# Postmix products with 112 weight columns, and the first loads of stage 1 moved into the last slots of attention

## The chip, the cores and the metric

The kernel runs on one core of one Trainium2 chip. The metric is the device time of one execution in microseconds (us); lower is better. A core has TensorE (PE for its products, PEld for its weight loads), VectorE (DVE), ScalarE (ACT), GpSimd (POOL) and SyncE (SP), each with an instruction queue that is worked off in order, and 16 DMA engines that all queues share.

## What is computed

Three layers, one after the other, on fp32 data (`w_in` and `w_out` of the second arrive as 64-bit floats):

```
scores = q @ k.T / 8                      # 4 batches, 12 heads, 448 x 448, head size 64
scores = einsum('bhij,hg->bgij', scores, w_pre)
attn   = softmax(scores, axis=-1)
attn   = einsum('bhij,hg->bgij', attn, w_post)
x      = (attn @ v) -> 1792 x 768
h = x @ w_in; g = h - tanh(h)             # 768 -> 2048
x = g @ w_out                             # 2048 -> 768
logits = x @ phi                          # 32 slots
d = softmax over tokens; slot_in = d.T @ x
slot_out[e] = relu(slot_in[e] @ w1[e]) @ w2[e]   # 8 experts, 4 slots each
out = softmax over slots(logits) @ slot_out
```

## The kernel before, in words

**Attention** (`talking_heads`) works on 16 chunks of 120 or 88 queries of one batch. A chunk's scores are computed per pair of heads (`scores`, L279) and copied to SBUF by ACT (`keep`, L287). A chunk is then cut into slots of 10 queries x 12 heads = 120 rows; there are 184 slots, and the loop at L579 takes one per turn of `s`. Two slots make a pair, and the work of a pair is:

- `regroup(s + 4)` (L304, on SP): a DMA that brings the score rows of one slot to the tile `D`, head by head. It is issued four slots, two pairs, ahead of its use, into one of six `D` buffers.
- `premix(s)` on even slots: products of `D` with `w_pre` (tile `pm`, L313), then the negated row maximum on DVE (`mx`, L317).
- `expo(s)`: exp on ACT with the row sums (`e`, L325); `guard`, `recip`, `norm`: POOL and DVE turn the sums into post-mixing weights `wk`, 60 columns for 12 heads x 5 queries (L331, L335, L342).
- `postmix(s - 4)`: products of `e` as weights with `wk` as moving operand (tile `tm`, L356). The result has keys on partitions. The 448 keys are 4 groups `c` of 112 (`JP`), and each group is cut in two halves `z` of 56 (`JH`), one at partition 0 and one at partition 64. So one product has 64 rows and 56 weight columns, and there are 2 x 4 x 2 x 2 = 32 per pair. An fp32 product is two instructions of TensorE, so that is 64 matmuls and 64 weight loads per pair. TensorE runs the four quarters of its array side by side.
- `gather(s - 1 - 4)` on odd slots: ACT copies `tm` to the tile `aT` (L370 to L374).
- `values` (tile `vx`, L395): products of `v` with `aT`; DVE copies `vx` to `xs` in `rest` (L405), which the loop puts behind the next `premix` (list `late`); a DMA takes `xs` to `xd` in HBM, input of stage 1.

Which slot gets the scores of a later chunk (`head`), the transposes of keys (`k_pair`, tile `kx`) and queries (`q_half`, tile `qx`), `values`, and loads is planned ahead of the loop from estimated loads per slot. Because `z` leaves gaps at partitions 56 to 63 and 120 to 127, the tiles for `v` (`vns`) and `tms` are set to zero there ahead of the loop (L536, L538 on DVE, L546 on POOL), and `load_v` needs two DMAs per half batch. Beside attention, `Conversion` turns `w_in` and most of `w_out` from 64-bit to 32-bit floats: a DMA into one of five `f64` buffers, steps on ACT, DVE and POOL (last a sum on POOL, L71), a store to HBM.

**Stage 1** (`moe_and_slots`) is a generator that attention starts as `follow()` at slot 180, after the pool of attention's early tiles is closed. It runs up to its next `yield` at each `next(more)`. The first run (end of slot 180) issues loads of four units of `w_in` (`load_w`, L776, 384 KB each) and of `x` (`load_x`, L819, three parts). The next runs come between the last postmixes and gathers: `split_w(0)` and `split_x` cut fp32 into two parts (ACT copy and DVE subtraction, L787, L788, L823, L824), five products that only keep TensorE busy (`warm`, L1197), then the products of step 0 (`product`, tile `hp`, L840) two column groups at a time, and the gate (`gate_act`, `gate_first`, `gate_last`). `save_w` stores split weights through ACT's queue (L801). From step 2 on each of 64 steps has 18 products, and weights of the experts are loaded as buffers come free; the last 80 us run the experts and the output.

Of the kernel before, what the change touches and what calls it, by code (L numbers as in the profile page):

```python
# [17 lines left out]
NP = NH // 2  # L18
NR = 4
JP = SEQ // NR  # L20
JH = JP // 2
IH = 5
# [51 lines left out]
class Conversion:  # L74
    def __init__(self, nc, w_in, w_out, wi, wo):
        self.nc, self.w_in, self.w_out, self.wi, self.wo = nc, w_in, w_out, wi, wo
        self.KD = w_in.shape[0] // 128
        self.CV = w_out.shape[1] // 2
        self.pool = None
        self.bufs = 5  # L80
        self.adder = nc.gpsimd
        self.t = {}

    def load(self, j):
        f, hf, o = j
        r = self.pool.tile([128, self.CV, 2], I32, tag="f64", name="f64", bufs=self.bufs)
# [46 lines left out]
def talking_heads(tc, ident, q, k, v, w_pre, w_post, xd, box, follow):  # L133
# [17 lines left out]
    er = early_stack.enter_context(tc.tile_pool(name="at_early", bufs=2))  # L151
    cv.pool = er
    psq = early_stack.enter_context(tc.tile_pool(name="at_psq", bufs=2, space=PSUM))

# [6 lines left out]
    def load_k(b, p):  # L161
        t = er.tile([JP, 2, NR, HD], FP32, tag="kn", name="kn", bufs=NP)
        nc.sync.dma_start(out=t, in_=k[b, 2 * p:2 * p + 2].rearrange("e (p r) d -> p e r d", r=NR))
        nat_k[b, p] = t

    def load_v(b, hf):
        t = vns[(2 * b + hf) % 3]
        src = v[b, hf * NP:(hf + 1) * NP].rearrange("h (p r) d -> p h r d", r=NR)
        for z in range(2):
            nc.sync.dma_start(out=t[64 * z:64 * z + JH], in_=src[JH * z:JH * z + JH])  # L170
        nat_v[b, hf] = t
# [175 lines left out]
    def postmix(s):  # L347
        es, wks = e_t.pop(s), wk_t.pop(s)
        xs = tms
        for x in range(2):  # L350
            for c in range(NR):
                for i in range(2):
                    for z in range(2):
                        h = slice(64 * i, 64 * i + 64)
                        j = JP * c + JH * z
                        nc.tensor.matmul(  # L356
                            xs[i][64 * z:64 * z + JH, x, c], lhsT=es[x][h, j:j + JH], rhs=wks[x][h],
                            start=True, stop=True)
        tm_t[s] = xs

    def gather(s):
        for i, x in enumerate(tm_t.pop(s)):
# [3 lines left out]
            c0 = sum(z for q, z in chunks[n][3] if q < o)  # L366
            out = attn_t[n].rearrange("p r h i -> p (r h) i")
            x = x.rearrange("p x r h i -> p (r h) x i")
            if m == 2 * IH:
# [14 lines left out]
    def values(n, g):  # L384
# [6 lines left out]
        for i in range(2):  # L391
            for c in range(NR):
                for e in range(2):
                    h = 4 * g + 2 * i + e
                    nc.tensor.matmul(  # L395
                        x[64 * e:64 * e + 64, i, :ni], lhsT=nat_v[b, h // NP][:, h % NP, c, :], rhs=a[:, c, h, :ni],
                        start=(c == 0), stop=(c == NR - 1))
# [136 lines left out]
    tms = [ps.tile([128, 2, NR, NH, IH], FP32, tag=f"t{i}", name="tm", bufs=1) for i in range(2)]  # L534
    for z in range(2):
        nc.vector.memset(vns[0][64 * z + 32:64 * z + 64], 0.0)  # L536
    for t in tms:
        nc.vector.memset(t, 0.0)  # L538

    for p in range(3, NP):  # L540
        load_k(0, p)
    for t in ds:
        nc.gpsimd.memset(t[:4], 0.0)
    for t in vns[1:]:
        for z in range(2):
            nc.gpsimd.memset(t[64 * z + 32:64 * z + 64], 0.0)  # L546
    for _ in range(WARM):
# [23 lines left out]
    for a in at.get(("head", -1), []):  # L571
        for f in scores4(*a):
            f()
    halves = []
    late = []
# [3 lines left out]
    while s < NS:  # L579
# [38 lines left out]
        for f in box["setup"][s - 6:s - 5] if s >= 6 else []:  # L618
            f()
        if s == NS - D_AHEAD:  # L620
            early_stack.close()
            more = follow()
            next(more)
# [19 lines left out]
def moe_and_slots(tc, ident, xd, wi, wo, wo4, wis, consts, w1, w2, out, box):  # L643
# [33 lines left out]
    psums = ExitStack()  # L677
    keep = whole.enter_context(tc.tile_pool(name="m_keep", bufs=1, reuse_waits="tile"))
    rgp = whole.enter_context(tc.tile_pool(name="m_ring", bufs=1, reuse_waits="tile"))
    xap = whole.enter_context(tc.tile_pool(name="m_xa", bufs=1, reuse_waits="tile"))  # L680
    xep = firsts.enter_context(tc.tile_pool(name="m_xe", bufs=1, reuse_waits="tile"))
    ph = psums.enter_context(tc.tile_pool(name="m_h", bufs=1, space=PSUM))
    bank_pool = {"h0": ph, "h1": ph}

# [3 lines left out]
    def r32(ap):  # L688
        return ap.bitcast(F32R)

    ceK = keep.tile([128, NBL, NSL], FP32, tag="ceK", name="ceK")
# [4 lines left out]
    rg = rgp.tile([128, 2 * RU], FP32, tag="rg", name="rg")  # L696
    rgs = rgp.tile([128, 2 * RU], FP32, tag="rgs", name="rg")
    xbuf = {0: [xap.tile([128, XW], FP32, tag=f"x{l}", name="xa") for l in range(2)]}
    quad, quad_a, quad_b = [xep.tile([128, FB * NRM], FP32, tag=f"quad{i}", name="quad") for i in range(3)]
    ring = [w.rearrange("p (m h i) -> p m h i", m=2, h=2) for w in (rg[:, :RU], rg[:, RU:], rgs[:, :RU], rgs[:, RU:])]  # L700

    def unit(t):
        return ring[t % 4] if t < THREE else ring[(4, 0, 1)[(t - THREE) % 3]]

# [93 lines left out]

    def save_w(t):
        if t < NF:  # L800
            nc.scalar.dma_start(out=wis[t], in_=unit(t))  # L801

# [6 lines left out]
    def load_x(p):  # L809
# [6 lines left out]
        dst = dst.rearrange("p (a s) -> p a s", a=KD)  # L816
        step = KD if p else 2
        for a in range(0, KD, step):
            nc.sync.dma_start(out=dst[:, a:a + step], in_=xd[p][:, a:a + step])  # L819

# [274 lines left out]
    def step(t):  # L1095
# [75 lines left out]
        if b == NPASS - 2 and f == NF - 1:  # L1171
            mem["slow"] = True
            for l in range(2):
                give(xap.tile([128, EXB], FP32, tag=f"x{l}", name="ex"))
        if b == NPASS - 1:
# [300 lines left out]
def fused_kernel(  # L1476
# [40 lines left out]
    def side(hf):  # L1517
# [14 lines left out]
        "late": [j for j in order if j[2] and j[0] >= LATE],  # L1532
    }
    with tc.manual_schedule():
        talking_heads(
# [31 lines left out]
```

## Time and profile before

| what | us |
|---|---|
| median of 3 runs (lowest, highest) | 891.73 (885.24, 895.21) |
| the profiled execution | 886.23 |
| its span, first to last instruction | 884.5 |
| attention up to the last premix | 0 to 434 |
| last postmixes and values, begin of stage 1 | 434 to 458 |
| steps of stage 1 | 458 to 775 |
| slots and experts | 775 to 884 |

The profile is of one execution; all rows below are of that one. Busy times of TensorE contain the time in which a product passes through the array: a group of 64 short matmuls begins one every few ns, each takes some 0.2 us. In rows of products, 64*56 is rows x weight columns, and 64x60 the moving operand.

### The profile page before, as it was taken

To read this page: it belongs to the slowest core of one execution; us is meant where nothing else is said; L and a number is where in the kernel's file an instruction comes from. 1 tells how busy PE (TensorE), PEld (TensorE's weight loads), DVE (VectorE), ACT (ScalarE), POOL (GpSimd) and SP (SyncE) were. 2 spreads that over 40 slices of the span, in tenths; PEclk is the share of its full clock that TensorE was granted. 3 is DMA by queue.
4 is the path that set the end of the run, shared out by engine and by line. 5 is a ranking of instruction groups with operands and counts; after the bars stand their busy time and mean duration, and the time that the engine had idled before them with its cause. 6 is when DMAs were issued, how large, how long until landed. Compare 5 with 4: busy or idle time off the path is not lost.

```text
span 884.5 us, 28648 instructions
## 1 busy us (share of the span) xinstructions
PE 807.9 (91%) x11790; PEld 570.8 (65%) x11790; DVE 556.7 (63%) x1181; ACT 570.5 (64%) x1345; POOL 247.7 (28%) x428
## 2 busy tenths in 40 slices
PE   8889988799987999899899999999999999999965
PEld 6556665566665667566676667667776786964322
DVE  5357766577666777788456986566765777830104
ACT  4777887687776878798666776546664666821103
POOL 5234344334334444454303452000000003700000
PEclk9999999899999999999999999999999999999988
DMA  9787888768888788785759976678764457899998
GB/s 182 191 234 220 213 236 248 218 190 211 231 253 226 219 206 239 236 254 177 256 176 363 374 260 223 207 316 317 302 215 175 149 179 256 313 359 413 424 392 303
DMA packets 131766, 224.53 MB, mean 254 GB/s; under 512 B 44852, under 2 KB 112436, under 8 KB 128052
## 3 DMA queue, kind: packets, MB, share of 16 engines
q1 hardware_dynamic: 128288, 209.84, 74.8%
q10 hardware_dynamic: 3348, 12.87, 3.7%
q8 instruction: 93, 1.52, 0.7%
q14 instruction: 37, 0.30, 0.1%
HBM read 147.96 MB, written 36.18 MB: 208 GB/s over the span
## 4 chain that ended last, share of the span: by engine, by line
PE 50%; DMA 18%; ACT 13%; DVE 12%; issue 5%; SPq 1%; POOL 1%; ACTq 0%; POOLq 0%; DVEq 0%
PE hp L840 21%; DMA D<-S 7%; DMA ex<-in_moe_w_dram 7%; ACT e L325 6%; PE pm L313 5%; PE sc L279 5%; DVE mx L317 4%; PE vx L395 3%; PE tm L356 3%; PE gt L911 2%; ACT S L287 2%; PE kx L236 2%; PE lgp L995 2%; PE sp L1077 1%; ACT aT L370 1%
## 5 line engine op out<-in xcount | busy, mean ns | idle before, releaser
L325 ACT ACTIVATE e<-pm,mx 128x448 f32<-128x448 f32 x184 | 115.1, 631 | 86.3 <-DVE mx L317 84.9
L840 PE MATMUL hp<-xa,rg 128*128 128x512 f32 x576 | 152.7, 405 | 0.2 <-POOL rg L788 0.2
L317 DVE TENSOR_REDUCE mx<-pm 128x1 f32<-128x448 f32 x184 | 106.1, 618 | 73.5 <-PE pm L313 73.4
L356 PEld LDWEIGHTS tm<-wk,e 64*56 64x56 f32 x5888 | 104.7, 128 | 62.8 <-issue 32.4
L356 PE MATMUL tm<-wk,e 64*56 64x60 f32 x5888 | 113.5, 216 | 13.3 <-issue 7.9
L313 PE MATMUL pm<-D,wpre 64*64 64x448 f32 (+2 forms) x736 | 107.6, 565 | 18.4 <-DMA D<-S 15.2
L840 PEld LDWEIGHTS hp<-xa,rg 128*128 128x128 f32 x576 | 102.3, 188 | 28.9 <-issue 10.5
L287 ACT ACTIVATE S<-sc 120x448 f32<-120x448 f32 (+1 forms) x186 | 91.4, 553 | 4.6 <-PE sc L279 3.0
L279 PE MATMUL sc<-khi,qT 64*120 64x448 f32 (+1 forms) x384 | 83.6, 392 | 9.3 <-DVE xs L405 6.2
L342 POOL TENSOR_SCALAR wk<-wpost,rv 128x60 f32<-128x60 f32 x184 | 86.9, 503 | 16.5 <-DVE rv L335 13.8
L331 POOL TENSOR_SCALAR rv<-ss 128x2 f32<-128x2 f32 x92 | 24.5, 266 | 225.3 <-ACT e L325 194.6
L395 PE MATMUL vx<-aT,vn 128*64 128x120 f32 (+1 forms) x1536 | 83.9, 262 | 2.0 <-ACT S L287 1.3
L797 POOL TENSOR_TENSOR rg<-rg 128x384 fp32r<-128x384 f32 x24 | 23.9, 1012 | 208.8 <-DVE rg L794 205.0
L395 PEld LDWEIGHTS vx<-aT,vn 128*64 128x64 f32 x1536 | 74.7, 137 | 7.2 <-issue 3.0
L860 ACT ACTIVATE sq<-hp 128x512 f32<-128x512 f32 (+1 forms) x62 | 32.9, 530 | 68.0 <-PE hp L840 68.0
L370 ACT ACTIVATE aT<-tm 128x480 f32<-128x480 f32 x144 | 75.8, 593 | 0.1
L871 DVE SCALAR_TENSOR_TENSOR qd<-qd,sq 128x512 f32<-128x512 f32 (+1 forms) x61 | 37.6, 616 | 59.1 <-ACT mk L867 53.7
L840 PE MATMUL hp<-xb,rg 128*128 128x512 f32 x288 | 74.7, 404 | 0.0
L840 PEld LDWEIGHTS hp<-xb,rg 128*128 128x128 f32 x288 | 52.1, 188 | 16.6 <-issue 6.3
L279 PEld LDWEIGHTS sc<-khi,qT 64*120 64x120 f32 (+1 forms) x384 | 45.3, 173 | 26.1 <-PE tm L356 9.4
L71 POOL TENSOR_TENSOR fa<-fa,f 128x384 f32<-128x384 f32 x56 | 57.7, 1030 | 6.4 <-DVE f L66 2.1
L313 PEld LDWEIGHTS pm<-D,wpre 64*64 64x64 f32 (+2 forms) x736 | 23.9, 132 | 51.4 <-DMA D<-S 23.2
(199 smaller groups left out, 1391.3 us busy)
## 6 DMA issues: line engine op xcount, KB each, us to landing
ex<-in_moe_w_dram SPq DMA_DIRECT2D x21, 1536.0 KB
D<-S SPq DMA_DIRECT2D x144, 210.0 KB
rg<-wis SPq DMA_DIRECT2D x36, 768.0 KB
f<-in_moe_w_in_dram SPq DMA_DIRECT2D x32, 384.0 KB
wis<-rg ACTq DMA_DIRECT2D x16, 768.0 KB
f<-in_moe_w_out_dram SPq DMA_DIRECT2D x24, 384.0 KB
rg<-wi SPq DMA_DIRECT2D x19, 384.0 KB
wi<-fa SPq DMA_DIRECT2D x32, 192.0 KB
```

The lines of the kernel that those rows point to most:

```text
L71: eng.tensor_tensor(out=out, in0=bits(a), in1=bits(p), op=ALU.add)
L279: nc.tensor.matmul(xs[e][0][:ni], lhsT=qT[n][s, l, p, :ni], rhs=kt[s], start=(i == 0), stop=(i == 2))
L287: nc.scalar.activation(out=dst, in_=xs[e][0][:ni], func=ACTF.Copy)
L313: nc.tensor.matmul(xs[x][64 * i:64 * i + 64], lhsT=wpre[k0:k1], rhs=d[i][k0:k1], start=True, stop=True)
L317: nc.vector.tensor_reduce(out=mx[:, x:x + 1], in_=xs[x], op=ALU.max, axis=AX.X, negate=True)
L325: nc.scalar.activation(out=es[x], in_=xs[x], func=ACTF.Exp, bias=mx[:, x:x + 1], accum_out=ss[:, x:x + 1])
L342: nc.gpsimd.tensor_scalar(out=wk, in0=wpost, scalar1=rv[:, x:x + 1], scalar2=None, op0=ALU.mult)
L356: nc.tensor.matmul(xs[i][64 * z:64 * z + JH, x, c], lhsT=es[x][h, j:j + JH], rhs=wks[x][h], start=True, stop=True)
L370: nc.scalar.activation(out=out[:, :, c0:c0 + m].rearrange("p a (x i) -> p a x i", x=2), in_=x, func=ACTF.Copy)
L395: nc.tensor.matmul(x[64 * e:64 * e + 64, i, :ni], lhsT=nat_v[b, h // NP][:, h % NP, c, :], rhs=a[:, c, h, :ni], start=(c == 0), stop=(c == ...
L840: nc.tensor.matmul(hp, lhsT=r32(w[:, m, hl, cs]), rhs=r32(x_of(b, c, l)), start=(c == 0 and i == 0), stop=(c == KD - 1 and i == 2))
L871: nc.vector.scalar_tensor_tensor(out=qd, in0=qd, scalar=TG_E, in1=sq, op0=ALU.add, op1=ALU.mult)
```

## The change

The postmix takes all 112 keys of a group as weight columns: 64 rows by 112 columns, 16 products per pair, at partitions 0 to 111. `gather` and `values` work on 112 partitions, `load_v` is one DMA, and the zeroing of `vns` and `tms` goes.

Stage 1's buffers `rg`, `rgs` and `xl` move to a pool `homes` that is open from the start. During attention `rgs` holds the keys as loaded (`kn`, six parts of one tile instead of six buffers), and `xl` four of the five `f64` buffers. The generator is started at slot 165: at slots 165, 167, 169 and 171 it issues one load of a `w_in` unit each, at 173, 175 and 177 one part of `x` each; the pools of stage 1 are opened at slot 180 as before. The splits of `w` unit 0 and of `x` part 0 go to slot 181, of `x` parts 1 and 2 to slot 183, and the products of step 0 follow the last postmixes one run earlier. The five `warm` products at that place go, and the stores of units 0 and 1 go through SP's queue.

```diff
@@ talking_heads
+    kns = box["homes"].tile([128, NP * 2 * NR * HD], FP32, tag="rgs", name="kn")
+    cv.place(box["homes"].tile([128, 4 * 2 * cv.CV], FP32, tag="xl", name="f64"))
...
     def load_v(b, hf):
         t = vns[(2 * b + hf) % 3]
         src = v[b, hf * NP:(hf + 1) * NP].rearrange("h (p r) d -> p h r d", r=NR)
-        for z in range(2):
-            nc.sync.dma_start(out=t[64 * z:64 * z + JH], in_=src[JH * z:JH * z + JH])
+        nc.sync.dma_start(out=t[:JP], in_=src)
...
@@ postmix
         for x in range(2):
             for c in range(NR):
                 for i in range(2):
-                    for z in range(2):
-                        h = slice(64 * i, 64 * i + 64)
-                        j = JP * c + JH * z
-                        nc.tensor.matmul(
-                            xs[i][64 * z:64 * z + JH, x, c], lhsT=es[x][h, j:j + JH], rhs=wks[x][h],
-                            start=True, stop=True)
+                    h = slice(64 * i, 64 * i + 64)
+                    nc.tensor.matmul(
+                        xs[i][:JP, x, c], lhsT=es[x][h, JP * c:JP * c + JP], rhs=wks[x][h], start=True, stop=True)
...
-    for z in range(2):
-        nc.vector.memset(vns[0][64 * z + 32:64 * z + 64], 0.0)
-    for t in tms:
-        nc.vector.memset(t, 0.0)
...
-    for t in vns[1:]:
-        for z in range(2):
-            nc.gpsimd.memset(t[64 * z + 32:64 * z + 64], 0.0)
...
+    first_load = NS - D_AHEAD - 15
...
+        if s == first_load:
+            more = follow()
+        if s >= first_load and (s - first_load) % 2 == 0 and s < first_load + 14:
+            next(more)
         if s == NS - D_AHEAD:
             early_stack.close()
-            more = follow()
+            next(more)
+        if s in (NS - 3, NS - 1):
             next(more)
@@ moe_and_slots
+    for t in range(4):
+        load_first(t)
+        yield
+    xl = rgp.tile([128, XW], FP32, tag="xl", name="xa")
+    for a in range(0, KD, 2):
+        nc.sync.dma_start(
+            out=xl.rearrange("p (a s) -> p a s", a=KD)[:, a:a + 2], in_=xd[0][:, a:a + 2])
+        yield
...
-    for t in range(4):
-        load_w(t)
-        if t == 0:
-            load_x(0)
     yield
     split_w(0, nc.vector)
-    save_w(0)
-    idle = bank("h1", [128, 128], "warm")
-    for _ in range(5):
-        nc.tensor.matmul(idle, lhsT=ident, rhs=ident, start=True, stop=True)
-    for i in range(0, KD, 2):
-        for c in range(i, i + 2):
-            split_x(0, c)
-        yield
-        product(0, {}, i, i + 2)
+    save_w(0, nc.sync)
+    split_x(0, 0)
+    yield
+    split_x(0, 1)
+    split_x(0, 2)
+    yield
+    product(0, {}, 0, 2)
+    split_x(0, 3)
+    split_x(0, 4)
+    yield
+    product(0, {}, 2, 4)
+    split_x(0, 5)
+    yield
+    product(0, {}, 4, KD)
+    yield
     split_w(1, nc.vector)
-    save_w(1)
+    save_w(1, nc.sync)
```

## Rows read from the trace of the kernel before

**Rows 1.** The page: engines' busy time, and its group of products of scores
```profile
PE 807.9 (91%) x11790; PEld 570.8 (65%) x11790; DVE 556.7 (63%) x1181; ACT 570.5 (64%) x1345; POOL 247.7 (28%) x428
...
L279 PE MATMUL sc<-khi,qT 64*120 64x448 f32 (+1 forms) x384 | 83.6, 392 | 9.3 <-DVE xs L405 6.2
```

**Rows 2.** Windows: attention from its first premix, its end, the passage to stage 1
```profile
core 0: us, PE busy (x) PEld busy (x) DVE busy (x) ACT busy (x) POOL busy (x), PEclk, DMA share, GB/s
22.00:433.60 411.60, 369.87 (x8732) 263.77 (x8732) 279.58 (x650) 323.69 (x854) 167.67 (x337) 0.99 0.80 221
400.00:433.60 33.60, 31.29 (x858) 22.84 (x853) 22.20 (x50) 25.59 (x71) 14.78 (x32) 1.00 0.58 172
433.60:452.10 18.50, 15.73 (x359) 13.28 (x357) 9.17 (x18) 12.22 (x31) 1.93 (x6) 1.00 0.73 255
```

**Rows 3.** Waits of TensorE, 22 to 434 us: us in total, times, longest
```profile
PE pm L313 <- DMA D<-S: 15.2, 10, 3.9
PE sc L279 <- DVE xs L405: 6.2, 14, 0.6
PE tm L356 <- issue: 5.4, 6, 2.3
```

**Rows 4.** Groups of instructions by form, TensorE: busy us, mean ns of one, idle before
```profile
L356 PE MATMUL tm<-wk,e 64*56 64x60 f32 x5888 | 113.5, 216 | 13.3 <-issue 7.9 <-ACT aT L370 2.2 <-ACT fa L50 1.0
L356 PEld LDWEIGHTS tm<-wk,e 64*56 64x56 f32 x5888 | 104.7, 128 | 62.8 <-issue 32.4 <-POOL fa L71 10.8 <-POOL wk L342 8.2
...
L279 PEld LDWEIGHTS sc<-khi,qT 64*120 64x120 f32 x288 | 34.7, 181 | 17.4 <-PE tm L356 6.7 <-issue 2.7 <-PE sc L279 1.8
...
L984 PE MATMUL wq<-seld,ex 96*128 96x32 f32 x32 | 4.2, 275 | 0.0
```

**Rows 5.** Timeline of TensorE in stage 1, a group with 128 weight columns
```profile
481.65 1.05 PE L984 MATMUL wq<-seld,ex 96*128 96x32 f32 x8
```

**Rows 6.** Timeline of two pairs: start us, us, what
```profile
342.12 0.98 PE L313 MATMUL pm<-D,wpre 64*64 64x448 f32 x8
...
342.93 1.03 PE L356 MATMUL tm<-wk,e 64*56 64x60 f32 x64
...
344.35 1.86 PE L395 MATMUL vx<-aT,vn 128*64 128x120 f32 x32
...
346.14 0.98 PE L313 MATMUL pm<-D,wpre 64*64 64x448 f32 x8
...
347.15 1.42 PE L356 MATMUL tm<-wk,e 64*56 64x60 f32 x64
...
347.18 1.16 DVE L317 TENSOR_REDUCE mx<-pm 128x1 f32<-128x448 f32 x2 [0.16 <-PE pm L313]
...
348.25 0.57 DVE L405 COPY xs<-vx 128x240 f32<-128x240 f32 x1
...
348.97 0.63 PE L279 MATMUL sc<-klo,qT 64*120 64x448 f32 x2
...
350.35 0.98 PE L313 MATMUL pm<-D,wpre 64*64 64x448 f32 x8
```

**Rows 7.** Timeline of TensorE from the last premix to the last values
```profile
433.62 0.98 PE L313 MATMUL pm<-D,wpre 64*64 64x448 f32 x8
...
437.48 1.31 PE L356 MATMUL tm<-wk,e 64*56 64x60 f32 x55 [0.20 <-ACT aT L374]
441.30 0.36 PE L356 MATMUL tm<-wk,e 64*56 64x60 f32 x9 [2.51 <-issue]
441.60 1.38 PE L1197 MATMUL warm<-ident 128*128 128x128 f32 x10
...
448.26 3.86 PE L395 MATMUL vx<-aT,vn 128*64 128x88 f32 x96
```

**Rows 8.** Timelines of POOL and DVE: last sum of a conversion, begin of the kernel
```profile
419.91 1.01 POOL L71 TENSOR_TENSOR fa<-fa,f 128x384 f32<-128x384 f32 x1
...
7.67 0.63 DVE L245 TENSOR_TENSOR klo<-kx,khi 128x448 fp32r<-128x448 f32 x1 [2.21 <-ACT khi L241]
...
26.29 0.23 POOL L331 TENSOR_SCALAR rv<-ss 128x2 f32<-128x2 f32 x1 [6.15 <-ACT e L325]
```

More of the change, by code (lines that the diff above doesn't have):

```diff
@@ L20 @@
 JP = SEQ // NR
-JH = JP // 2
 IH = 5
@@ L82, in __init__, with place @@
         self.t = {}
+        self.loads = 0
+    def place(self, x):
+        n = x.shape[1] // 4
+        self.raw = [x[:, i * n:(i + 1) * n] for i in range(4)]
+        self.raw += [self.pool.tile([128, n], FP32, tag="f64", name="f64", bufs=1)]
     def load(self, j):
         f, hf, o = j
-        r = self.pool.tile([128, self.CV, 2], I32, tag="f64", name="f64", bufs=self.bufs)
+        r = self.raw[self.loads % self.bufs].bitcast(I32).rearrange("p (f w) -> p f w", w=2)
+        self.loads += 1
         if o:
@@ L161, in load_k @@
     def load_k(b, p):
-        t = er.tile([JP, 2, NR, HD], FP32, tag="kn", name="kn", bufs=NP)
+        n = 2 * NR * HD
+        t = kns[:JP, p * n:(p + 1) * n].rearrange("p (e r d) -> p e r d", e=2, r=NR)
         nc.sync.dma_start(out=t, in_=k[b, 2 * p:2 * p + 2].rearrange("e (p r) d -> p e r d", r=NR))
@@ L366, in gather @@
             c0 = sum(z for q, z in chunks[n][3] if q < o)
-            out = attn_t[n].rearrange("p r h i -> p (r h) i")
-            x = x.rearrange("p x r h i -> p (r h) x i")
+            out = attn_t[n][:JP].rearrange("p r h i -> p (r h) i")
+            x = x[:JP].rearrange("p x r h i -> p (r h) x i")
             if m == 2 * IH:
@@ L395, in values @@
                     nc.tensor.matmul(
-                        x[64 * e:64 * e + 64, i, :ni], lhsT=nat_v[b, h // NP][:, h % NP, c, :], rhs=a[:, c, h, :ni],
+                        x[64 * e:64 * e + 64, i, :ni], lhsT=nat_v[b, h // NP][:JP, h % NP, c, :], rhs=a[:JP, c, h, :ni],
                         start=(c == 0), stop=(c == NR - 1))
@@ L677, in moe_and_slots @@
     psums = ExitStack()
[L678 to L683, printed above, removed]
+    rgp = box["homes"]
+    bank_pool = {}
     def bank(tag, shape, name):
@@ L689, in r32, with unit, load_first @@
         return ap.bitcast(F32R)
+    rg = rgp.tile([128, 2 * RU], FP32, tag="rg", name="rg")
+    rgs = rgp.tile([128, 2 * RU], FP32, tag="rgs", name="rg")
+    ring = [w.rearrange("p (m h i) -> p m h i", m=2, h=2) for w in (rg[:, :RU], rg[:, RU:], rgs[:, :RU], rgs[:, RU:])]
+    def unit(t):
+        return ring[t % 4] if t < THREE else ring[(4, 0, 1)[(t - THREE) % 3]]
+    def load_first(t):
+        nc.sync.dma_start(out=unit(t)[:, :, 1], in_=wi[t].rearrange("p (m i) -> p m i", m=2))
+    for t in range(4):
[6 more added lines that the diff above has]
+        yield
+    keep = whole.enter_context(tc.tile_pool(name="m_keep", bufs=1, reuse_waits="tile"))
+    xap = whole.enter_context(tc.tile_pool(name="m_xa", bufs=1, reuse_waits="tile"))
+    xep = firsts.enter_context(tc.tile_pool(name="m_xe", bufs=1, reuse_waits="tile"))
+    ph = psums.enter_context(tc.tile_pool(name="m_h", bufs=1, space=PSUM))
+    bank_pool.update(h0=ph, h1=ph)
     ceK = keep.tile([128, NBL, NSL], FP32, tag="ceK", name="ceK")
@@ L694, in moe_and_slots @@
     wphi = keep.tile([128, NF, NSL], FP32, tag="wphi", name="wphi")
-    rg = rgp.tile([128, 2 * RU], FP32, tag="rg", name="rg")
-    rgs = rgp.tile([128, 2 * RU], FP32, tag="rgs", name="rg")
-    xbuf = {0: [xap.tile([128, XW], FP32, tag=f"x{l}", name="xa") for l in range(2)]}
+    xbuf = {0: [xap.tile([128, XW], FP32, tag="x0", name="xa"), xl]}
     quad, quad_a, quad_b = [xep.tile([128, FB * NRM], FP32, tag=f"quad{i}", name="quad") for i in range(3)]
-    ring = [w.rearrange("p (m h i) -> p m h i", m=2, h=2) for w in (rg[:, :RU], rg[:, RU:], rgs[:, :RU], rgs[:, RU:])]
-    def unit(t):
-        return ring[t % 4] if t < THREE else ring[(4, 0, 1)[(t - THREE) % 3]]
     def by_column(e):
@@ L797, in split_half, with save_w @@
             nc.gpsimd.tensor_tensor(out=r32(l), in0=l, in1=h, op=ALU.subtract)
-    def save_w(t):
+    def save_w(t, eng=nc.scalar):
         if t < NF:
-            nc.scalar.dma_start(out=wis[t], in_=unit(t))
+            eng.dma_start(out=wis[t], in_=unit(t))
     def x_of(p, c, l):
@@ L816, in load_x @@
         dst = dst.rearrange("p (a s) -> p a s", a=KD)
-        step = KD if p else 2
-        for a in range(0, KD, step):
-            nc.sync.dma_start(out=dst[:, a:a + step], in_=xd[p][:, a:a + step])
+        nc.sync.dma_start(out=dst, in_=xd[p])
     def split_x(b, c, eng=nc.vector):
@@ L1172, in step @@
             mem["slow"] = True
-            for l in range(2):
-                give(xap.tile([128, EXB], FP32, tag=f"x{l}", name="ex"))
+            give(xap.tile([128, EXB], FP32, tag="x0", name="ex"))
+            give(rgp.tile([128, EXB], FP32, tag="xl", name="ex"))
         if b == NPASS - 1:
@@ L1533, in fused_kernel @@
     }
+    box["homes"] = ctx.enter_context(tc.tile_pool(name="homes", bufs=1, reuse_waits="tile"))
     with tc.manual_schedule():
```

## Prediction

> **What bounds the kernel now.** I read the page first, then the windows by stage, TensorE's waits, its groups by form, and two pairs on the timeline. TensorE is busy for 91% of the span, far ahead of the next engine [rows 1]. In attention it is busy for 369.9 of 411.6 us, ACT for 323.7, DVE for 279.6, and the DMA engines for 0.80 of the time [rows 2]. So only 41.7 us of idle TensorE stand in this stretch, and their largest shares are 15.2 us in ten waits for a late `D` and 5.4 us in six holes in which the postmix had no instruction to run ("issue") [rows 3]. Attention goes at TensorE's pace with ACT close behind.
>
> One layer deeper the pairs are of two kinds. A pair without scores (342.12 to 346.14, 4.02 us) is products end to end: premix, postmix, a transpose, values [rows 6]. A pair with scores (346.14 to 350.35, 4.21 us) is set by a chain: the maximum ends at 348.3, only then does DVE copy `xs` out of a bank (348.25 to 348.82), and only then do the remaining scores run (348.97), 1.38 us before the next premix [rows 6]. There the postmix is beside the chain, not on it. The page has 384 products with `khi`, 8 per group of scores, so 48 groups [rows 1]; four of them come ahead of the loop, so 44 of the 92 pairs hold one (5888 postmix instructions by 64 [rows 4]).
>
> **Part 1: the postmix.** Removed: 32 of 64 matmuls and 32 of 64 weight loads per pair. What is left is dearer. Before, four products run side by side, so 64 instructions are 16 rounds. A group of 64 takes 1.03 us [rows 6], of which 0.216 is the passage of the last one [rows 4]: 0.81 over 15 rounds is 54 ns a round. After, only two fit side by side (two halves of 64 rows, all columns used), so 32 instructions are again 16 rounds, and the moving operand keeps its 60 columns. Halving the count saves no round.
>
> The weights then set the round. A load of 120 columns lasts 181 ns, one of 56 lasts 128 [rows 4]: 53 ns over 64 columns is 0.83 ns per column, on top of a fixed passage. What a stream of such loads costs, a group in stage 1 shows: 8 products with 128 weight columns and only 32 moving columns take 1.05 us [rows 5], less 0.275 for the last [rows 4], over 7 steps: 111 ns each, although 32 moving columns would need less than the 54 ns that 60 need. That is 128 columns by 0.83 plus 5. For 112 columns it makes 0.93 + 5, 98 ns. The form itself, two halves of 64 rows with 112 columns and a short moving operand, stands nowhere in the trace. Bounds for a round: below, 27 ns (if the number of instructions were what costs), or 54 (if loads hide); above, 2 x 111 = 222 ns, if the two halves' loads go one after the other. Against that end stand the four loads of 56 columns which now fit into one round of 54 ns: side by side they must be, one after the other they need 4 x 47. I take 98, the nearest row. A postmix then lasts 15 x 98 + 216 = 1.69 us, 0.66 more; its first load is longer too, by up to 0.05 where nothing hides it. I take +0.68.
>
> Where it counts. In the 48 pairs without scores TensorE has no gap, so the whole 0.68 is on the path: +33 us. In the 44 with scores the postmix begins 0.8 after the premix and would end by 0.8 + 1.66 = 2.5 us; the remaining scores begin at 2.83 as before. There it is covered; in some the gap is smaller, and I put +2 us. If that cover were gone, the 44 cost +30. The wait that makes the second pair's postmix 1.42 instead of 1.03 us [rows 6] is for ACT's copies `aT` of the pair before; as that pair gets longer and ACT's work doesn't, it should go.
>
> What gives back. A slower pace loads the DMA engines less and gives each `D`, issued two pairs ahead, about 1 us more: ten waits by 1.0 is -10. The six holes for instructions should shrink with a quarter of TensorE's 23,580 instructions gone (5,888): -3. Between nothing and all 20.6 us of the two, I take -13.
>
> A rule that speaks against the change stands in the Trainium skill, "TensorEngine Tiling (Array Packing)", Key Properties: going from one tiling mode to another drains TensorE. Premix and postmix now share 64 x 64; after the change the postmix shares its mode with scores instead, so in pairs without scores one switch more appears. From postmix to the next kind it is 0.96 us now (342.93 to 343.89) against 0.81 of rounds, so a switch is at most 0.15, of which up to 0.1 is the next one's weight load. By the rule the sum would rise by 48 x 0.05 to 0.15, 2 to 7 us; without it, nothing. I leave it to the range.
>
> Gather and values keep their element counts per partition, so their time. `load_v` moves the same bytes with one issue instead of two: nothing, either way below 1 us per load. The zeroing is hidden today: DVE's first use after it waits 2.21 us for ACT, and POOL is idle for 6.15 us after its own [rows 8]. It saves nothing. Keys and `f64` as slices of one tile: nothing if each slice waits for its own readers, as the halves of `rg` do already; if whole tiles waited, keys of the next batch would come late three times, some us each.
>
> **Part 2: the loads and splits.** From the last premix (433.62) to the end of the last values (448.26 + 3.86) it is 18.5 us, of which TensorE is idle 2.8: mostly one hole of 2.51 us in the postmix, marked "issue", while the seven loads fill the DMA engines [rows 2, 7]. Five `warm` products add 1.38, some 1.2 of it alone [rows 7]. With the loads spread over slots 165 to 177, where the DMA engines are at 0.58 [rows 2], the hole and the warm products go: -4 us. What is late next is the last gather's copies, ahead of the values, some 0.3 us. The seven issues lie in SP's queue behind a regroup each and ahead of the next. The last conversion's sum (419.91 to 420.92 [rows 8]) falls, counting pairs back from the last premix, in slot 174, and its `f64` buffer lies where the load of slot 173 writes; SP waits there 2 to 3 us with the regroup of slot 178 behind it, which has 7 to 8 us of lead. Cost 0 to 2 us; I take 0. Splits in slots 181 and 183 (some 3 us on ACT and DVE together) stand in front of the maximum and exp of the last pair, in gaps: in this passage ACT is busy 12.2 and DVE 9.2 of 18.5 us [rows 2]. Nothing, at most 1 us. Stage 1 then starts earlier as a whole.
>
> **The sum.** 886.2 + 33 + 2 - 13 - 4 = 904. The three runs lie from 885.2 to 895.2 around the profiled 886.2, with the median 5.5 above; I say 906.
>
> **The rivals.**
> A. Paid in every pair: the chain doesn't cover it, because the postmix delays all that follows in TensorE's order. 92 x 0.70 = 64, less 5 and 4: 942. For it: TensorE is at 90% in attention. Against: the two pairs of rows 6.
> B. Mostly swallowed: many pairs without scores hold a wait longer than 0.68, so some 24 pay: +16 - 13 - 5 = 884, same as before. For it: 41.7 us of idle time and ACT at 79%. Against: pairs as the first of rows 6, without a gap.
> C. Loads hide after all (54 ns a round): only the holes and the passage count, -4 to -8: 880.
> D, the other side. The number of instructions is the price. Now it is 1.03 / 64 = 16 ns each; half as many would halve a postmix's 0.81: -0.4 in 48 pairs, -20, and -4: 862. It decides if a round stays under 54 ns. Against: 64 instructions in 16 rounds already move at the moving operand's pace, and 111 ns in rows 5. The Trainium skill's page just named, section "Instruction Overhead", states some 60 cycles for each matmul, whatever its length; so read, the postmix would fall to half. Hanging on that sentence: the trace doesn't agree, 16 ns is less than 60 cycles at 2.4 GHz (25 ns).
> That the earlier loads do harm (late `D` in the last slots) would give back the 4.
>
> **How the numbers follow.** Forecast 0.60, its own range 892 to 920; A 0.13; B 0.15; C 0.07; D 0.05. A measurement here tells about 1% from no change: below 882.8 or above 900.6. Faster: D, half of C, a little of B: 0.12. Within: the rest of B and C, and the quarter of the forecast's case in which more is given back: 0.29. Slower: the rest, 0.59. The range 880 to 940 leaves out D, part of C, and the upper half of A.
>
> **What would show it.** Right: a postmix of 32 matmuls lasting about 1.7 us, loads of 112 columns near 170 ns, matmuls in twos about 98 ns apart; pairs without scores near 4.7 us, those with scores still 4.2; less waiting for `D`; no hole after 437 and 16 us from last premix to last values. Wrong: a postmix of 1.0 us or less, or pairs with scores that also grow by 0.6.

## The result, and the profile after

The change makes the kernel slower by a little under one per cent: ratio 1.0078 [1.0054, 1.0102], with a median of 896.5 us (14 runs) against 887.6 us of the kernel before (14 runs). All ratios leave out runs in a slower state, which the medians contain: two of these 14 (903.5 and 906.6 us), four of `e7_halfpost`, one of `e2_part1`, and one of `e1_part2` that took 1085 us. The forecast was 906, slower by 1.6%. The sign came out as said, the size at half, and the whole lies within the 1% that the prediction called no change. The profiled execution took 892.6 us (span 890.9), 6.4 more than that of before, and this is the difference that the lines below explain.

The page of the kernel after, engines' busy time, for [rows 1]:
```profile
PE 855.1 (96%) x8836; PEld 614.9 (69%) x8836; DVE 553.4 (62%) x1177; ACT 571.2 (64%) x1345; POOL 243.0 (27%) x424
```
Its groups by form (busy us, mean ns of one, idle before), for [rows 4]:
```profile
L362 PE MATMUL tm<-wk,e 64*112 64x60 f32 x2944 | 165.0, 261 | 0.8 <-ACT aT L375 0.8
L362 PEld LDWEIGHTS tm<-wk,e 64*112 64x112 f32 x2944 | 152.6, 174 | 64.9 <-POOL wk L350 35.2 <-issue 16.0 <-POOL fa L70 7.7
```
TensorE runs a quarter fewer instructions and is busy 47 us longer: half as many postmix products, each with twice the weights. The idle time before them, 13.3 us before, is 0.8.

Its windows, attention from its first to its last premix, then the passage to the end of the last values, for [rows 2]:
```profile
22.00:439.80 417.80, 412.89 (x5886) 305.19 (x5885) 280.30 (x651) 326.21 (x858) 168.81 (x339) 1.00 0.79 223
439.80:456.70 16.90, 16.90 (x253) 14.03 (x251) 8.81 (x17) 10.97 (x28) 1.37 (x4) 1.00 0.30 110
```
Attention: busy +43.0 us (369.9 to 412.9), idle -36.8 (41.7 to 4.9), sum +6.2. Passage: 18.5 to 16.9, so -1.6. The rest, from there to the end of the span, is 434.2 instead of 432.4 (+1.8): not explained, and within what single executions differ by. Together 6.4. That the dearer products added 43 us of busy time and only 6 of them are seen is the finding to be explained.

The granted clock of the two stretches, 0.99 and 1.00, hides one more difference. In the kernel before, TensorE was granted half its clock (0.50, so 1.2 instead of 2.4 GHz) in two stretches of attention, 10.2 us together:
```profile
47.10:50.50 3.40, 3.40 (x54) 2.51 (x47) 2.19 (x6) 3.01 (x8) 1.43 (x4) 0.50 0.80 204
166.60:173.40 6.80, 4.74 (x81) 3.65 (x83) 2.71 (x6) 2.23 (x7) 0.65 (x2) 0.50 0.74 227
```
One began just behind a wait of 2.2 us for `D`, the other within the longest one:
```profile
168.66 1.02 PE L313 MATMUL pm<-D,wpre 64*64 64x448 f32 x3 [3.94 <-DMA D<-S]
```
The kernel after has no such stretch in attention. The 8.1 us of busy time in them would be about half as long at the full clock, so some 4 us of work went along with the waits (an estimate from these rows).

Its waits of TensorE, 22 to 440 us (us in total, times, longest), all that the view names; [rows 3] are those of before:
```profile
PE pm L321 <- DMA D<-S: 2.9, 7, 0.6
PE tm L362 <- ACT aT L375: 0.8, 1, 0.8
PE pm L321 <- POOL wk L350: 0.6, 1, 0.6
PE sc L287 <- issue: 0.4, 1, 0.4
```
The same view of the kernel before has these rows too, which the prediction did not weigh:
```profile
PE kx L236 <- ACT S L287: 2.9, 6, 0.9
PE pm L313 <- ACT e L325: 2.5, 4, 0.8
PE tm L356 <- ACT aT L370: 2.2, 5, 0.8
PE sc L279 <- DVE klo L245: 1.5, 6, 0.3
```
The late `D` and the holes are nearly gone, as was said, but so are the short waits for DVE and ACT: 6.2 for `xs`, 9.1 in the four rows above, and two smaller ones of 1.3 and 1.0, together 17.6 us, of which 0.8 are left.

Its timeline of TensorE over two pairs (start us, us, what), for [rows 6]:
```profile
340.57 0.98 PE L321 MATMUL pm<-D,wpre 64*64 64x448 f32 x8
341.48 1.79 PE L362 MATMUL tm<-wk,e 64*112 64x60 f32 x32
...
345.44 0.98 PE L321 MATMUL pm<-D,wpre 64*64 64x448 f32 x8
346.36 1.78 PE L362 MATMUL tm<-wk,e 64*112 64x60 f32 x32
...
348.28 0.63 PE L287 MATMUL sc<-klo,qT 64*120 64x448 f32 x2
...
349.65 0.98 PE L321 MATMUL pm<-D,wpre 64*64 64x448 f32 x8
```
The pair without scores takes 345.44 - 340.57 = 4.87 us (4.02 before). The pair with scores takes 4.21, as before: there the longer postmix is covered by the maximum and the copy `xs`.

Its timeline of the passage, for [rows 7]:
```profile
439.76 1.50 PE L321 MATMUL pm<-D,wpre 64*64 64x448 f32 x8
441.19 1.78 PE L362 MATMUL tm<-wk,e 64*112 64x60 f32 x32
...
446.58 3.07 PE L855 MATMUL hp<-xa,rg 128*128 128x512 f32 x12
449.57 1.78 PE L362 MATMUL tm<-wk,e 64*112 64x60 f32 x32
...
452.89 3.86 PE L400 MATMUL vx<-aT,vn 112*64 112x88 f32 x96
```
The hole of 2.51 us and the `warm` products are gone, and stage 1's products (`hp`) stand between the last postmixes.

### The profile page after: what moved, and what is told of

Same layout as the page of the kernel before. It is cut to its first block, busy times and chain, and to the rows that moved or that the text cites. A ratio compares the mean times of both kernels' runs of the same rounds, so it can differ in the third digit from the quotient of the medians.

```text
span 890.9 us, 22716 instructions
## 1 busy us (share of the span) xinstructions
PE 855.1 (96%) x8836; PEld 614.9 (69%) x8836; DVE 553.4 (62%) x1177; ACT 571.2 (64%) x1345; POOL 243.0 (27%) x424
## 3 DMA queue, kind: packets, MB, share of 16 engines
q8 instruction: 70, 1.15, 0.5%
## 4 chain that ended last, share of the span: by engine, by line
PE 74%; DMA 12%; DVE 6%; ACT 3%; issue 3%; POOL 0%; SPq 0%; ACTq 0%; POOLq 0%; DVEq 0%
PE hp L855 21%; PE tm L362 15%; PE pm L321 9%; PE vx L400 8%; PE sc L287 7%; DMA ex<-in_moe_w_dram 7%; DMA D<-S 5%; PE kx L244 2%; PE gt L926 2%; PE lgp L1010 2%; PE sp L1092 1%; PE qx L266 1%; PE h L1351 1%; PE wt L979 1%; PE si L1316 1%
## 5 line engine op out<-in xcount | busy, mean ns | idle before, releaser
L362 PEld LDWEIGHTS tm<-wk,e 64*112 64x112 f32 x2944 | 152.6, 174 | 64.9 <-POOL wk L350 35.2
L362 PE MATMUL tm<-wk,e 64*112 64x60 f32 x2944 | 165.0, 261 | 0.8 <-ACT aT L375 0.8
L321 PE MATMUL pm<-D,wpre 64*64 64x448 f32 (+2 forms) x736 | 102.4, 561 | 3.7 <-DMA D<-S 2.9
L400 PE MATMUL vx<-aT,vn 112*64 112x120 f32 (+1 forms) x1536 | 83.3, 262 | 0.0
L287 PE MATMUL sc<-khi,qT 64*120 64x448 f32 (+1 forms) x384 | 77.3, 382 | 0.8 <-DVE qT L270 0.8
L400 PEld LDWEIGHTS vx<-aT,vn 112*64 112x64 f32 x1536 | 74.2, 137 | 5.0 <-issue 2.1
L375 ACT ACTIVATE aT<-tm 112x480 f32<-112x480 f32 x144 | 75.8, 591 | 0.2
L855 PEld LDWEIGHTS hp<-xb,rg 128*128 128x128 f32 x288 | 52.1, 189 | 16.9 <-issue 6.4
L287 PE MATMUL sc<-klo,qT 64*120 64x448 f32 (+1 forms) x192 | 46.3, 374 | 0.4 <-issue 0.4
```

What stands on the lines that cost most here:

```text
L287: nc.tensor.matmul(xs[e][0][:ni], lhsT=qT[n][s, l, p, :ni], rhs=kt[s], start=(i == 0), stop=(i == 2))
L321: nc.tensor.matmul(xs[x][64 * i:64 * i + 64], lhsT=wpre[k0:k1], rhs=d[i][k0:k1], start=True, stop=True)
L362: nc.tensor.matmul(xs[i][:JP, x, c], lhsT=es[x][h, JP * c:JP * c + JP], rhs=wks[x][h], start=True, stop=True)
L375: nc.scalar.activation(out=out[:, :, c0:c0 + m].rearrange("p a (x i) -> p a x i", x=2), in_=x, func=ACTF.Copy)
L400: nc.tensor.matmul(x[64 * e:64 * e + 64, i, :ni], lhsT=nat_v[b, h // NP][:JP, h % NP, c, :], rhs=a[:JP, c, h, :ni], start=(c == 0), stop=( ...
L855: nc.tensor.matmul(hp, lhsT=r32(w[:, m, hl, cs]), rhs=r32(x_of(b, c, l)), start=(c == 0 and i == 0), stop=(c == KD - 1 and i == 2))
```

## The experiments

Two theories stood against each other. By the first, the pace (Theory 1 in the expectations): attention is a set of nearly balanced loops (TensorE 370, ACT 324, DVE 280 us busy, DMA engines at 0.80 [rows 2]), TensorE's stalls are lateness of the others, and whatever slows TensorE by some tenths of a us per pair gives them time to catch up, so that a dearer product mostly replaces waits. By the second, the count (Theory 3 there): it was the number of TensorE's instructions that fell, and with it the holes for instructions and what they delay. Beside these stands the question what each of the two parts does alone (Theory 2 there: part 2, with its other buffers, took the waits away). All ratios are to the kernel before, with 95% intervals.

**Each part alone.** `e1_part2` has the loads and splits of the change with the postmix of before; `e2_part1` has the postmix of the change alone.
```diff
 # e1_part2, against the kernel after (zeroing and two loads of v as before)
-                    h = slice(64 * i, 64 * i + 64)
-                    nc.tensor.matmul(xs[i][:JP, x, c], lhsT=es[x][h, JP * c:JP * c + JP], ...
+                    for z in range(2):
+                        h = slice(64 * i, 64 * i + 64)
+                        j = JP * c + JH * z
+                        nc.tensor.matmul(xs[i][64 * z:64 * z + JH, x, c], lhsT=es[x][h, j:j + JH], ...
 # e2_part1: the same hunk the other way, against the kernel before
```


> The loads and splits of stage 1 as in the changed kernel, the postmix as before (64 rows by 56 columns, two loads of v, the zeroing). Theory 1 (the slower postmix itself, by its slower pace, took the waits away): the ten waits for D come back, 10 to 18 us of TensorE idle for D in attention; only the passage to stage 1 gets shorter, by about 4 us, so 0.995 of before, some 883. Theory 2 (part 2, with its other buffers, took the waits away): under 5 us of waits for D, attention some 12 us shorter, 0.98 of before, some 870.

> The postmix of 64 rows by 112 columns alone, loads and splits of stage 1 as before. Theory 1: attention as in the changed kernel, under 8 us of TensorE idle in it, pairs without scores at 4.88 us; the hole in the passage may come back; 1.012 of before, some 899. Theory 2: the waits for D stay, 12 to 18 us of idle in attention, 1.025 of before, some 910.

Measured: `e1_part2` 888.7 us, 0.9991 [0.9954, 1.0029]; `e2_part1` 894.9 us, 1.0049 [1.0017, 1.0081], less than the 1.012 expected. What slows the kernel is the postmix. In `e2_part1` attention has the idle time of the kernel after, 417.5 - 413.0 = 4.5 us, without any of part 2:
```profile
22.00:439.50 417.50, 412.97 (x5884) 306.98 (x5884) 280.24 (x651) 325.87 (x857) 168.82 (x339) 0.99 0.78 219
```
In `e1_part2` the waits stay as in [rows 3], so Theory 2 falls (waits of TensorE, 22 to 438 us):
```profile
PE pm L323 <- DMA D<-S: 14.9, 10, 2.4
PE tm L366 <- issue: 3.7, 4, 2.5
```
Part 2 by itself gains nothing, and its trace says where the gain goes. The passage is 3.0 us shorter:
```profile
438.10:453.60 15.50, 15.05 (x347) 12.21 (x347) 8.80 (x17) 10.98 (x28) 1.37 (x4) 1.00 0.34 124
```
But it begins at 438.1 instead of 433.6, and 3.5 of these 4.5 us are lost in the last ten pairs, where the premixes wait for `D` (TensorE, start us, us):
```profile
427.92 0.93 PE L323 MATMUL pm<-D,wpre 64*64 64x448 f32 x2 [0.94 <-DMA D<-S]
429.48 0.60 PE L323 MATMUL pm<-D,wpre 64*64 64x448 f32 x3 [0.62 <-DMA D<-S]
...
438.06 1.33 PE L323 MATMUL pm<-D,wpre 64*64 64x448 f32 x5 [0.77 <-DMA D<-S]
```
The same stretch of SP's queue has the loads of `xa` between the regroups:
```profile
423.37 1.71 SPq L314 DMA_DIRECT2D D<-S  x2
425.13 0.94 SPq L718 DMA_DIRECT2D xa<-xd  x1
...
431.96 0.81 SPq L718 DMA_DIRECT2D xa<-xd  x1
432.88 1.59 SPq L314 DMA_DIRECT2D D<-S  x2
```
The transfers that filled the passage now stand among the last regroups of attention. That they are what makes these late is a reading of the order; `e8_late_x` below tests it.

With the wide postmix part 2 has even less to give. In `e2_part1`, without it, the passage holds no hole either:
```profile
439.50:457.10 17.60, 17.60 (x263) 14.83 (x261) 8.88 (x17) 11.48 (x28) 1.42 (x4) 1.00 0.68 228
```
Part 2 takes 0.7 us more from it (16.9 in the kernel after). The last ten pairs took 3.5 us more than before in `e2_part1` and 4.3 in the kernel after, so the loads cost some 0.8 there: nothing is left.

**The postmix cut in another way.** `e3_split64` keeps the layout of the change (keys on 112 contiguous partitions) and cuts each product into 64 and 48 weight columns, so that four run side by side again.
```diff
-                    h = slice(64 * i, 64 * i + 64)
-                    nc.tensor.matmul(xs[i][:JP, x, c], lhsT=es[x][h, JP * c:JP * c + JP], ...
+                    for z0, z1 in ((0, 64), (64, JP)):
+                        h = slice(64 * i, 64 * i + 64)
+                        nc.tensor.matmul(xs[i][z0:z1, x, c], lhsT=es[x][h, JP * c + z0:JP * c + z1], ...
```


> The changed kernel with each product of 112 columns cut into 64 and 48 columns, at partitions 0 and 64, so that four run side by side again and keys still lie on partitions 0 to 111. If the weight load sets the round, 64 columns need 0.93 per column plus 5, 53 + 5 = 58 ns a round, against 52.5 to 54 if the moving operand sets it; a postmix lasts 1.08 us. Theory 1: the waits come back with the pace (10 to 18 us for D), 0.993 of before, some 881. Theory 2: under 5 us of waits, 0.975, some 866.

Measured: 886.3 us, 0.9966 [0.9928, 1.0003]. A postmix takes 1.10 us instead of 1.78; the starts of its products lie 58 to 59 ns apart where the weights have 64 columns and 52 to 53 where they have 48. So the 98 ns are the price of the wide load, not of the new layout. (The expectation's "0.93 per column" should read 0.83; its 53 + 5 is worked out with that.) With the pace of before the waits are back; those for `D` are fewer than the 10 to 18 us expected, and the time is above the 0.993 expected (TensorE, 22 to 435 us):
```profile
PE pm L321 <- DMA D<-S: 7.9, 6, 2.6
PE tm L363 <- issue: 6.5, 7, 1.8
PE sc L287 <- issue: 5.7, 5, 1.6
```
`e9_split64_only`, the same cut on `e2_part1`, without part 2:

> The postmix cut into 64 and 48 columns on 112 partitions, one load of v, no zeroing, and nothing of part 2. As fast a postmix as before (58 and 53 ns a round) with as many instructions, so 0.998 to 1.003 of before. If it is clearly below 1, the single load of v or the shape gives something that I have put at nothing.

Measured: 887.5 us, 0.9984 [0.9958, 1.001]: not to be told from before, nor from `e3_split64`.

**Pace or count.** `e4_twice` has every postmix product of before twice (the second writes the same values). `e6_longmove` keeps the number of instructions but lets 48 of the 64 products of a pair move 120 columns instead of 60; the surplus is overwritten by the next. `e7_halfpost` is `e2_part1` with two of the four key groups only, so key groups 2 and 3 are left out of the result.
```diff
 # e4_twice, against the kernel before
-        for x in range(2):
+        for x in (0, 1, 0, 1):
 # e6_longmove, against the kernel before
+                        w = wks[x][h]
+                        n = 2 if c < NR - 1 else 1
                         nc.tensor.matmul(
-                            xs[i][64 * z:64 * z + JH, x, c], lhsT=es[x][h, j:j + JH], rhs=wks[x][h],
-                            start=True, stop=True)
+                            xs[i][64 * z:64 * z + JH, x, c:c + n], lhsT=es[x][h, j:j + JH],
+                            rhs=w.unsqueeze(1).to_broadcast([64, n, NH, IH]), start=True, stop=True)
 # e7_halfpost, against e2_part1
-            for c in range(NR):
+            for c in range(2):
```


> The kernel before with every product of the postmix issued twice into the same place (the output is the same): 128 matmuls in some 1.9 us, as slow as the changed kernel's postmix (1.7 to 1.8) with four times its instructions. Theory 1 (pace): waits for D under 5 us, pairs with scores 4.2 to 4.4, pairs without scores about 4.9, 1.01 to 1.025 of before, 897 to 910. Theory 3 (the waits went because a quarter of the instructions went): the waits stay and the holes for instructions double to some 10 us or more, 1.04 or more, 925 and up.

> The kernel before with the moving operand of the postmix read twice (120 columns) for three of the four key groups; the second copy is overwritten by the next group, so the output is the same. The same 64 matmuls and 64 weight loads per pair as before, but 12 of 16 rounds last about 102 instead of 53 ns: a postmix is 0.6 us longer, near the changed kernel's. Theory 1 (the pace took the waits away): TensorE's waits for D fall below 6 us and those for DVE and ACT below 5, and the time is 1.00 to 1.01 of before. Theory 3 (fewer instructions took them away): D waits stay at 10 us or more and holes for instructions stay; 1.03 or more, 915 and up. A mixture: D, DVE and ACT waits go, holes for instructions stay at 5 to 10 us.

> The changed postmix (64 rows by 112 columns) without part 2, for two of the four key groups only; the other two are left out of the result. 8 rounds of 98 ns per pair, so TensorE is as fast as before (about 0.8 us from first to last start) with a quarter of the postmix's instructions. Theory 1 (pace): the waits for D come back, 10 to 18 us, pairs with scores stay at 4.2, pairs without scores 4.0; 0.98 to 1.0 of before, the gain being only the holes for instructions. Theory 3 (count): waits under 8 us in all, attention 25 us or more shorter, 0.97 or less, under 862.

`e4_twice`: 1001.9 us, 1.1264 [1.1209, 1.132], far above the 1.01 to 1.025 of the pace and within the open "1.04 or more" of the count. The late `D` are gone, as the pace has it and the count does not, but the holes for instructions take their place. The window of attention:
```profile
22.00:546.00 524.00, 444.84 (x14432) 347.44 (x14432) 280.66 (x651) 330.61 (x856) 166.39 (x339) 0.96 0.63 180
```
Waits of TensorE, 22 to 546 us:
```profile
PE tm L356 <- issue: 44.9, 37, 3.9
PE sc L279 <- issue: 14.3, 10, 3.1
PE vx L395 <- issue: 12.4, 6, 4.6
...
PE pm L313 <- DMA D<-S: 0.5, 1, 0.5
```
TensorE idles 79 of 524 us, 77 of them in such holes. "issue" only says that the profile shows nothing that was waited for; the transfers of the instruction queue in the trace say what it was. All 57 of these holes end 1.1 to 1.8 us after such a transfer has ended, though the stretch holds only 114 transfers, and the seven holes of the kernel before end 1.3 to 1.6 us after one. So the second theory has something real in it: the supply of instructions is a limit of its own. The holes are not the whole of the 112 us that attention is longer: busy time grew by 75, and in 46.8 us of the stretch the granted clock was 0.50, against 10.2 in the kernel before.

`e6_longmove`: 893.8 us, 1.005 [1.002, 1.0079]. Its window of attention:
```profile
22.00:440.00 418.00, 404.48 (x8737) 313.00 (x8740) 279.63 (x651) 326.06 (x857) 167.79 (x339) 0.99 0.79 219
```
Its waits of TensorE, 22 to 440 us:
```profile
PE pm L313 <- DMA D<-S: 7.5, 6, 2.4
PE tm L358 <- issue: 1.8, 2, 0.9
```
One postmix on its timeline:
```profile
336.86 1.62 PE L358 MATMUL tm<-wk,e 64*56 64x120 f32 x64
```
As many instructions as before, a slower postmix (1.62 us instead of 1.03), idle time 13.5 us instead of 41.7, no wait for DVE left, and the same loss as `e2_part1`. The pace alone does most of it; half of the waits for `D` stay (7.5 us, where under 6 was expected).

`e7_halfpost`: 883.0 us, 0.9901 [0.9867, 0.9935]. Its profiled execution ran at a granted clock of 0.94 in attention and is read only for the kinds of waits (22 to 438 us):
```profile
PE pm L311 <- DMA D<-S: 11.5, 9, 2.7
PE sc L277 <- DVE xs L400: 10.0, 17, 0.8
```
A quarter of the instructions of the postmix of before in as much time (1.00 us against 1.03), no hole for instructions left, and the waits for `D`, DVE and ACT are back. So a small count removes the holes, not the other waits; those go with a slower pace. And the limit behind TensorE is near: half of the wide postmix, 0.78 us in each of 92 pairs or 72 us of TensorE, is gone against `e2_part1`, and the time is only 1.5% lower.

**The loads put elsewhere.** In `e8_late_x` (on `e3_split64`) and `e11_wide_late_x` (on the kernel after) the three loads of `xa`, issued in slots 173 to 177, go together in slot 179, and the first split of `x` comes two slots later.
```diff
-        if s >= first_load and (s - first_load) % 2 == 0 and s < first_load + 14:
+        if s >= first_load and (s - first_load) % 2 == 0 and s < first_load + 8 or s == NS - D_AHEAD - 1:
 ...
-        yield
+    yield
 ...
-    split_x(0, 0)
     yield
+    split_x(0, 0)
```


> The postmix cut into 64 and 48 columns, part 2 changed: the four loads of w_in at slots 165 to 171 as in the changed kernel, the three loads of x at slot 179, behind the last regroup, instead of 173 to 177; the first split of x two slots later. If the loads of x between the last regroups are what makes the last D late (2 to 3 us of waits in the last pairs and up to 3 us more in split premixes), the last pairs are back at 4.3 and 3.5 us and the passage stays short: 0.991 to 0.994 of before, some 882 to 884, against 0.9966 with the loads at 173 to 177. If the loads aren't the cause, 0.9966 again.

> The changed kernel with the three loads of x at slot 179 instead of 173 to 177 and the first split of x two slots later; postmix with 112 columns in all pairs. If the x loads between the last regroups are what keeps part 2 from helping, the last pairs lose their waits: 1.002 to 1.005 of before against the changed kernel's 1.0078 and 1.0049 for the postmix alone. If not, 1.007 again.

Measured: `e8_late_x` 884.8 us, 0.994 [0.991, 0.9969], against 0.9966 of `e3_split64`; the waits for `D` fall from 7.9 to 4.7 us and the last pairs have none. The intervals overlap, so the direction is as the reading of `e1_part2` wants it and the size is open; other holes differ too ("issue" 17.9 us in `e8_late_x`, 12.4 in `e3_split64`). `e11_wide_late_x` 891.9 us, 1.0062 [1.0033, 1.009]: above what was expected of it. With the wide product part 2 gives no gain that can be measured, in either place.

**Wide only where it is covered.** `e10_mixed` (on `e8_late_x`) takes the product of 112 columns in the pairs in which a group of scores starts, and 64 and 48 elsewhere.
```diff
+        covered = any(("head", now[0] + i) in at for i in range(2))
+        cuts = ((0, JP),) if covered else ((0, 64), (64, JP))
-                    for z0, z1 in ((0, 64), (64, JP)):
+                    for z0, z1 in cuts:
```


> As e8_late_x, but in the pairs in which a group of scores starts the postmix takes 112 columns in one product (32 matmuls), in all others 64 and 48 (64 matmuls). If the 0.7 us of a wide postmix are covered by the chain over the maximum and the copy of xs in pairs with scores, and holes for instructions grow with their number, pairs with scores stay at 4.2, the holes shrink by about a third, and the time is 0.985 to 0.992 of before, below e8_late_x's 0.994. If the cover doesn't hold, 44 x 0.7 = 30 us are added: 1.02 or more. If it holds but the holes don't depend on the number, 0.994 again.

Measured: 881.4 us, 0.9938 [0.9911, 0.9965]. A wide and a narrow pair on its timeline:
```profile
330.88 0.98 PE L321 MATMUL pm<-D,wpre 64*64 64x448 f32 x8
331.82 1.96 PE L365 MATMUL tm<-wk,e 64*112 64x60 f32 x30
...
335.23 0.98 PE L321 MATMUL pm<-D,wpre 64*64 64x448 f32 x8
336.03 1.10 PE L365 MATMUL tm<-wk,e 64*64 64x60 f32 x64
```
Counted from premix to premix, the 41 pairs with scores and no values beside them take 193.7 us in all (178.3 before) and the 47 without scores 197.5 (215.1 before). That is not the cover giving way: 8.2 of these 15.4 us lie in three pairs in which TensorE was granted half its clock, in two of them behind a late `D` (3.0 and 1.6 us):
```profile
47.00:53.80 6.80, 6.80 (x50) 5.01 (x50) 2.43 (x6) 3.01 (x8) 1.81 (x5) 0.50 0.81 187
...
251.80:258.60 6.80, 6.80 (x52) 5.07 (x56) 2.66 (x8) 3.80 (x9) 1.22 (x3) 0.50 0.85 260
```
The median pair with scores is 4.31 us against 4.21, so some 0.1 of the wide postmix's 0.75 shows. The holes for instructions shrink, to 5.5 us from 17.9 in `e8_late_x`, but the time misses the 0.985 to 0.992 expected of that. It can't be told apart from `e8_late_x`; both beat the kernel before by 0.6% and the changed one by some 1.4%.

## Why the prediction was right or wrong

**The price of a round: right.** Forecast 98 ns from 111 ns for 128 columns; the starts of the products lie 98 ns apart. The load was to last near 170 ns and lasts 174, the postmix 1.69 us and lasts 1.78. Rival C (loads hide) and rival D (the number is the price) fall with this: 16 rounds of 98 ns, not 32 products of 16 ns. The prediction's "0.93 + 5" stands for 93 + 5 ns. Of the Trainium skill's "Instruction Overhead" ("TensorEngine Tiling (Array Packing)"), named beside D, `e4_twice` says the same as the prediction: 128 products in 1.87 us are 15 ns each, less than 60 cycles. Four of them run side by side, so this speaks only against that price for one product after the other; what one tile pays it doesn't show.

**The price of a pair without scores: under-sized.** Forecast +0.68, measured +0.85 in the pairs shown (4.87 against 4.02; the commonest difference of all 47 is 0.86). The postmix itself is 0.75 longer, not 0.66, and 0.10 lies between the start of the premix and that of the postmix, 0.91 instead of 0.81. In `e10_mixed` the two forms stand in one kernel, 0.94 before the wide postmix and 0.80 before the narrow one. This is the place where the prediction weighed the drain at a change of mode (the Trainium skill, same page, Key Properties) and left it to the range at 0.05 to 0.15: the trace agrees with the rule in sign, but doesn't show its price alone, since the longer first load (174 instead of 128 ns) lies in the same 0.1 us. 47 pairs by 0.85 are 40 us, where the sum had 33.

**The cover in pairs with scores: right** for this kernel, 4.21 as before, so rival A falls. In `e10_mixed`, where the pairs between are quicker, about 0.1 us of a pair shows.

**"What gives back": the step that failed.** The prediction took -13 and called 20.6 us, the late `D` and the holes, the most there was. Measured from premix to premix, the 47 pairs without scores grew by 13.0 us (215.1 to 228.1): ten that had held a wait are shorter by 13.8 together, the other 37 longer by 26.7. The 41 with scores alone shrank by 6.3 (178.3 to 172.0), and the three that hold values too by 0.7. Against a gross price of 40 that is 34 given back. The two named waits fell by 17.3, not 13 (`D` 15.2 to 2.9, "issue" 5.4 to 0.4), and the half-clock stretches, which the prediction did not weigh, held some 4 (estimated above). What else was left out are short waits, 11.4 us for ACT and for `klo` of DVE, and the pairs with scores, which were put down as fixed by their chain at 4.2 though 15 of them held a stall, a late `D` among others, and gave 10 us back. The 6.2 us of waits for `xs` don't belong here: all stand in pairs with scores, five of which are as long as before to 0.01 us. There the longer postmix fills them; they are the cover, which the sum had at nothing already. The last few us of the 34 aren't put down to a cause. The bound of 20.6 was wrong because it listed the waits that had a story; the whole idle time of the stretch, 41.7 us, stood in the first window that the prediction quotes. `e6_longmove` shows that a slower TensorE alone removes most of it, and `e7_halfpost` that a smaller number of instructions does not. That the total of 906 still came within 10 us is in part luck: too low a price for the pairs without scores, by 7, took off some of what the give-back had wrong. Rival B, mostly swallowed, described what happened better than the forecast did; its sum of 884 gave too little for the dearer pairs.

**Part 2: -4 forecast, nothing measured.** The passage went as said: no hole, no `warm` products, in `e1_part2` -3.0 us (in the kernel after -1.6, with three dearer postmixes in it, of which the wide postmix alone has 0.9 in `e2_part1`). In `e1_part2` 3.5 us were lost again in the last ten pairs, by the order of SP's queue to the loads among the last regroups, which were taken at 0. In the kernel after it was some 0.8. The prediction named this ("late `D` in the last slots") and gave it no chance. Whether a longer lead for the regroups would cure it wasn't tried.

The +1.8 us between the passage and the end of the span stay open.

## What to carry to other kernels

Where the engines are nearly balanced, price a dearer instruction on the busiest one against all of that engine's idle time in the stretch, not against the waits that have a name; and by the same coin a saving there is mostly turned into waits (`e7_halfpost`: 72 us less of TensorE's work for 1.5%). Where a product's moving operand is short its weight load sets the rate, so cut the weights until as many products run side by side as fit (64 and 48 columns here, not 112). Before putting bulk loads between the last transfers that a loop waits for, to spare the stage behind it, count the queue that they pass (3.5 us lost for 3.0 gained in `e1_part2`, one trace).

## What the runs showed of the hardware that was not expected

The supply of instructions is a limit of TensorE: every hole of `e4_twice` ends 1.1 to 1.8 us after a transfer of the instruction queue. In attention, by the windows and waits above and of the kernel before:

| kernel | matmuls per us (as many loads) | idle for instructions, us |
|---|---|---|
| after | 14 | 0.4 |
| before | 21 | 6.1 |
| `e6_longmove` | 21 | 3.3 |
| `e3_split64` | 21 | 12.4 |
| `e4_twice` | 28 | 77 |

At three quarters of the last rate the holes are 3 to 12 us, and at that rate they are 15% of the stretch. The page's instruction queue moved 2.28 MB in `e4_twice`, 1.52 in the kernel before and 1.15 after.

A moving operand of twice the length costs as much as weights of twice the width: 64 products that mostly move 120 columns took 1.62 us (`e6_longmove`), its long rounds 102 ns apart, close to the 98 ns of 112 weight columns with 60 moving. Either side can set the round. With 60 moving columns the round is 52 to 53 ns for 48 weight columns, 58 to 59 for 64 and 98 for 112.

A late transfer can cost more than its wait. In or behind waits for `D` of 2.2 and 3.9 us in the kernel before, and of 3.0 and 1.6 in `e10_mixed`, the granted clock fell to 0.50 for 3.4 or 6.8 us. It needn't: a wait of 3.2 us that ended at 281.2 us in the kernel before left it at 1.
